# Second matmul with the weights stationary, evacuated by a transposing copy

## The chip, the cores and the metric

The kernel runs on one core of a Trainium2 chip. The metric is the device time of one execution in microseconds (us). Before the change three executions took 692.01, 692.06 and 692.52 us; the median is 692.06. TensorE (PE in the profile) multiplies, VectorE (DVE) and ScalarE (ACT) work elementwise, GpSimd (POOL) and SyncE (SP) mostly issue DMAs here. TensorE accumulates into PSUM[...]; the other tiles lie in SBUF.

## The reference

A causal convolution of 7 taps over the sequence, with weights shared within each of 8 heads, and then two matmuls with a leaky ReLU between them:

```python
# attention: x (8, 4096, 192), weight (8 heads, 7 taps)
w = softmax(weight, axis=-1)
out[b, s, h*24 + g] = sum_k w[h, k] * x_pad[b, s + k, h*24 + g]   # 6 zeros in front
# moe: tokens = out.reshape(32768, 192), w_in (192, 2048), w_out (2048, 192)
h = tokens @ w_in
g = np.maximum(0.01 * h, h)
return (g @ w_out).astype(np.float32)
```

## The kernel before

**Layout.** Two sequences are handled together: partitions 0 to 63 hold 64 channels of sequence `2*rp`, partitions 64 to 127 the same channels of `2*rp + 1`, and the 192 channels are three chunks c of 64. A block `blk` is 512 positions (`ST`) of such a pair, 1024 tokens; there are 32. The first four blocks (`NHALF`) are worked as two *half groups* of T = 256 positions each, the other 28 as one *full group* of T = 512: 36 groups, counted from 0. `xt` holds x with channels on partitions, `yt` the convolved x in the same layout, `g` the activated hidden layer with the 2048 hidden units on partitions in 16 pieces `fc` (`NFC`).

**Convolution.** `conv_jobs` gives 21 VectorE instructions per group, for each tap k and within it each chunk c: tap 0 a multiply (L187), taps 1 to 6 a multiply-add onto `yt` (L193). The last three jobs are thus tap 6 of chunks 0, 1 and 2, and a chunk of `yt` is ready when its tap 6 is done.

**First matmul.** `mm1(grp, u)` does one of 16 (full: one piece f) or 8 (half: two pieces) units of a group: for each chunk c and each sequence e a matmul with 64 rows and 128 columns of `w_in` stationary and T columns of `yt` moving (L403). The two e lie on different row halves of the array, so the pair runs side by side; I call it a round. The result `ph` (two buffers of two banks) is activated into `g` by ScalarE (L410).

**Second matmul.** It lags the first by a group. `mm2_slot(q)` issues one slot: two matmuls of 64 hidden units each (row tile `rt`), with `g` stationary and 192 columns of `w_out` moving (L429). A pair of 128-token outputs `po` takes 32 slots in two passes of 16, `rnd`; between the passes the two row tiles change banks, and `seal` is an instruction that waits for the last matmul of the first pass and for which the first of the second pass waits. `evac_o` copies a finished `po` to SBUF, on ScalarE for half groups and on VectorE for full ones (L476), and SyncE writes it to the output (L479, L484) in rows of 768 bytes. `psum_o` has four buffers, `po` among them. The last block's eight outputs are done at the end with 128 matmuls of the whole array.

**Order.** Every engine runs its instructions in the order in which the Python code issues them (`tc.manual_schedule()`). A group has T/64 steps: two units of `mm1`, then `quota[j]` slots; the convolution of the *next* group is dealt out over the steps, before a step's slots in full groups and after them in half groups:

```python
jobs = ahead[per * j : per * (j + 1)]
if T == ST:
    ...
    for job in jobs:
        job()
    jobs = []
for _ in range(quota[j]):
    mm2_slot(slot)
...
for job in jobs:
    job()
```

A half group has 4 steps of 6, 6, 6 and 3 jobs, a full one 8 steps of 2 or 3. `load_x` (L78, on GpSimd's queue) and `transpose_x` (L93, on SyncE's queue, which also carries the outputs) bring x into `xt` about two blocks ahead. The first two groups' x comes over a special path of TensorE transposes (L149, L156), and a few taps of the first groups are convolved on TensorE (L212).

## Time and profile before

| | |
|---|---|
| median of three executions | 692.06 us |
| the profiled execution | 692.51 us, of which 690.8 us are its span |
| TensorE busy / VectorE / ScalarE | 685.2 / 501.6 / 514.4 us |
| second matmul, L429 | 8064 matmuls, 387.9 us busy |
| first matmul, L403 | 3456 matmuls, 384.1 us busy |
| convolution, L193 and L187 | 735 instructions, 436.3 us busy |
| copies of the outputs, L476 | 224 on VectorE (80.1 us), 32 on ScalarE (10.2 us) |
| DMA | 53.79 MB, 78 GB/s |

Times in the profile are those of one execution. Busy time counts overlapping matmuls once per engine and the ends of matmuls are modelled, so the rows' mean durations are longer than the distance from one matmul to the next; the pace is read from starts in the timeline. Line numbers in what follows are those of the kernel before unless said otherwise.

### The profile page before, as it was taken

To read this page: it belongs to the slowest core of one execution; us is meant where nothing else is said; L and a number is where in the kernel's file an instruction comes from. 1 tells how busy PE (TensorE), PEld (TensorE's weight loads), DVE (VectorE), ACT (ScalarE), POOL (GpSimd) and SP (SyncE) were. 2 spreads that over 40 slices of the span, in tenths; PEclk is the share of its full clock that TensorE was granted. 3 is DMA by queue.
4 is the path that set the end of the run, shared out by engine and by line. 5 is a ranking of instruction groups with operands and counts; after the bars stand their busy time and mean duration, and the time that the engine had idled before them with its cause. 6 is when DMAs were issued, how large, how long until landed. Compare 5 with 4: busy or idle time off the path is not lost.

```text
span 690.8 us, 25914 instructions
## 1 busy us (share of the span) xinstructions
PE 685.2 (99%) x11708; PEld 584.0 (85%) x11708; DVE 501.6 (73%) x986; ACT 514.4 (74%) x569; POOL 148.0 (21%) x206
## 2 busy tenths in 40 slices
PE   9999999999999999999999999999999999999998
PEld 6999988888888888888888888888888888888887
DVE  5899666777777787777787777777777877777712
ACT  6888898777777777777777777777777777777771
POOL 6822222211222201222202222112222112000000
PEclk9999999999999999999999999999999999999999
DMA  9976656455565545565455566355565455322112
GB/s 151 117 93 94 82 69 84 80 78 70 75 85 82 76 77 75 66 94 82 71 78 71 74 84 88 67 78 75 77 82 80 77 75 66 67 60 59 48 42 64
DMA packets 184159, 53.79 MB, mean 78 GB/s; under 512 B 149104, under 2 KB 183664, under 8 KB 184048
## 3 DMA queue, kind: packets, MB, share of 16 engines
q0 software_dynamic: 99536, 14.76, 30.2%
q1 hardware_dynamic: 84512, 37.38, 22.8%
q8 instruction: 91, 1.49, 0.9%
q14 instruction: 20, 0.16, 0.1%
HBM read 29.88 MB, written 25.17 MB: 80 GB/s over the span
## 4 chain that ended last, share of the span: by engine, by line
PE 98%; ACT 2%; issue 0%; DVE 0%
PE po L429 49%; PE ph L403 47%; ACT g L410 2%; PE acc L212 1%; PE warm L284 1%; PE ptr L149 0%; ACT yt L371 0%; DVE o_sb L476 0%; PE ptr L156 0%; PE wps L320 0%; PE wps_l L320 0%; DVE zero L227 0%; DVE junk L229 0%
## 5 line engine op out<-in xcount | busy, mean ns | idle before, releaser
L410 ACT ACTIVATE g<-ph 128x1024 bf16<-128x1024 f32 x512 | 496.3, 1021 | 155.9 <-PE ph L403 155.4
L193 DVE SCALAR_TENSOR_TENSOR yt<-xt,wk,yt 128x512 bf16<-128x512 bf16 (+1 forms) x630 | 399.5, 691 | 0.2
L429 PEld LDWEIGHTS <-g 64*128 64x128 bf16 (+1 forms) x8064 | 361.9, 94 | 34.4 <-issue 0.2
L429 PE MATMUL po<-w_out,g 64*128 64x192 bf16 (+1 forms) x8064 | 387.9, 243 | 0.0
L403 PE MATMUL ph<-yt,w_in 64*128 64x512 bf16 (+1 forms) x3456 | 384.1, 352 | 1.5 <-ACT g L410 0.7
L403 PEld LDWEIGHTS <-w_in 64*128 64x128 bf16 x3456 | 226.0, 111 | 64.7 <-issue 3.7
L78 POOL DMA_DIRECT2D x_bf<-in_x_dram x180 | 134.6, 772 | 422.6 <-DMA xt<-x_bf 420.1
L476 DVE COPY o_sb<-po 128x192 f32<-128x192 f32 x224 | 80.1, 358 | 163.9 <-PE po L429 156.3
L187 DVE TENSOR_SCALAR yt<-xt,wk 128x512 bf16<-128x512 bf16 (+1 forms) x105 | 36.8, 381 | 12.8 <-DMA xt<-x_bf 12.6
L476 ACT COPY o_sb<-po 128x192 f32<-128x192 f32 x32 | 10.2, 320 | 1.5 <-PE po L429 0.2
L168 DVE COPY xt<-ptr 128x384 bf16<-128x384 bf16 x7 | 2.2, 354 | 6.9 <-PE ptr L156 4.5
L212 PE MATMUL acc<-xt,diag 64*64 64x256 bf16 x84 | 6.7, 327 | 0.0
L212 PEld LDWEIGHTS <-diag 64*64 64x64 bf16 x84 | 5.5, 133 | 1.3 <-DVE wk L366 0.4
L284 PE MATMUL warm<-zero 128*128 128x256 bf16 (+1 forms) x20 | 4.8, 405 | 1.1 <-DVE junk L229 1.1
L127 POOL DMA_DIRECT2D x_half<-in_x_dram x6 | 4.3, 714 | 3.2 <-DMA w_in<-in_moe_w_in_dram 3.2
L284 PEld LDWEIGHTS <-zero 128*128 128x128 bf16 x20 | 2.5, 136 | 2.1 <-DVE junk L229 1.1
L249 POOL DMA_DIRECT2D w_in<-in_moe_w_in_dram x6 | 3.9, 654 | 0.0
L371 ACT ACTIVATE yt<-acc,rsum 128x256 bf16<-128x256 f32 x3 | 1.4, 474 | 2.9 <-PE acc L212 2.9
L345 ACT ACTIVATE diag<-ident,whm 128x64 bf16<-128x64 bf16 x14 | 3.5, 335 | 0.0
L123 POOL DMA_DIRECT2D x_rows<-in_x_dram x4 | 2.9, 733 | 0.2 <-issue 0.2
L133 ACT CAST x_half<-x_nat 128x384 bf16<-128x384 f32 x2 | 1.0, 512 | 1.2 <-DMA x_nat<-in_x_dram 1.1
L290 ACT ACT_TABLE_LOAD x1 | 1.3, 1283 | 0.8 <-PEq L575 0.8
(37 smaller groups left out, 11.9 us busy)
## 6 DMA issues: line engine op xcount, KB each, us to landing
out_dram<-o_sb SPq DMA_DIRECT2D x117, 192.0 KB, 2.1
x_bf<-in_x_dram POOLq DMA_DIRECT2D x180, 64.0 KB, 3.2
out_dram<-o_sb SPq DMA_DIRECT2D x22, 96.0 KB, 1.6
xt<-x_bf SPq DMA_TRANSPOSE x90, 2.5
w_in<-in_moe_w_in_dram POOLq DMA_DIRECT2D x4, 192.0 KB, 5.8
w_in<-in_moe_w_in_dram POOLq DMA_DIRECT2D x2, 384.0 KB, 9.4
w_out<-in_moe_w_out_dram POOLq DMA_DIRECT2D x1, 768.0 KB, 11.2
x_nat<-in_x_dram SPq DMA_DIRECT2D x2, 192.0 KB, 2.6
```

What stands on the lines that cost most here:

```text
L78: nc.gpsimd.dma_start(out=t[:, c, :, e, :], in_=src[2 * rp + e, :, :, c * CH : (c + 1) * CH],)
L127: nc.gpsimd.dma_start(out=x_half[q][:, c, :, e, :], in_=rows[:, e, :, c * CH : (c + 1) * CH],)
L187: lambda s=src, d=dst, c=c: nc.vector.tensor_scalar_mul(d, s, wk[:, c, 0:1])
L193: lambda s=src, d=dst, c=c, k=k: nc.vector.scalar_tensor_tensor(out=d, in0=s, scalar=wk[:, c, k : k + 1], in1=d, op0=mybir.AluOpType.mult, ...
L212: lambda k=k, p=p, a=a, e=e, ps=ps: nc.tensor.matmul(out=acc[ps, :T], lhsT=diag[c][ps, p, k, :], rhs=xt[0][ps, c, a : a + T], start=(k == ...
L249: nc.gpsimd.dma_start(out=w_in[n][e * CH : (e + 1) * CH], in_=moe_w_in[:, fs].rearrange("(c p) f -> p c f", p=CH),)
L284: nc.tensor.matmul(out=wa[:, 0, 0:cols], lhsT=zero[:, 0:128], rhs=zero[:, 0:cols], start=True, stop=True,)
L345: nc.scalar.activation(out=diag[c][:, p, k, :], in_=ident2, func=mybir.ActivationFunctionType.Copy, scale=whm[:, c, p, k : k + 1],)
L403: nc.tensor.matmul(out=ph[:, e, i * T : (i + 1) * T], lhsT=w_in_of(f, ps, c), rhs=y[ps, c, t0 : t0 + T], start=(c == 0), stop=(c == NCH - 1),)
L410: act = nc.scalar.activation(out=g[blk][:, nf * u : nf * (u + 1), :, t0 : t0 + T], in_=ph.rearrange("p e (i t) -> p i e t", i=nf), func=my ...
L429: return nc.tensor.matmul(out=po[m], lhsT=g[b][ps, fc, e, s * 128 : (s + 1) * 128], rhs=w_out[ps, fc, :], start=start, stop=stop,)
L476: ins = copy(out=o_sb[:, n % 2, :], in_=po.pop(n))
```

## The change

The second matmul now keeps 64x64 pieces of `w_out` stationary and moves T columns of `g`. A slot issues four matmuls, for the two halves of the hidden piece (`rt`) and the two sequences (`e`), each on its own 64x64 quarter of the array. The output is transposed: `acc2[gi, r]` has on partition `64*e + m` the output channel `3*m + r` (`NR` = 3) of sequence e and T positions in a row. A group takes three passes of 16 slots, 48 in all; the two row tiles are always on different r, r = 1 is finished after the second pass, r = 0 and r = 2 after the third. After passes one and two `seal`, now always a ScalarE copy of one element, lies between.

`evac_t` takes an `acc2` to SBUF with VectorE's transposing copy of 32x32 blocks, into a tile `o_t` that has positions on partitions; with the third, four DMAs write the group's output in runs of 96 channels (384 bytes). The first matmul's matmuls are split in two of 64 columns each (`h`), so that both matmuls use the same 64x64 tiles. `g_pool` goes from three buffers to two. The quotas are written out: half groups 16, 16, 8, 8; full groups 5, 5, 6, 5, 5, 6, 8, 8; groups 6 to 8 have their own. The last block keeps its matmuls.

```diff
-    g_pool = ctx.enter_context(tc.tile_pool(name="g", bufs=3))
+    g_pool = ctx.enter_context(tc.tile_pool(name="g", bufs=2))
...
-                    nc.tensor.matmul(
-                        out=ph[:, e, i * T : (i + 1) * T],
-                        lhsT=w_in_of(f, ps, c),
...
+                    for h in range(2):
+                        nc.tensor.matmul(
+                            out=ph[h * CH : (h + 1) * CH, e, i * T : (i + 1) * T],
+                            lhsT=w_in_of(f, ps, c, h),
...
+    def w_out_of(ps, fc, r):
+        return w_out[ps, fc, r::NR]
 
     def mm2_slot(q):
...
-        p, fc = divmod(q, 2 * NFC)
+        gi, fc = divmod(q, NR * NFC)
         rnd, fc = divmod(fc, NFC)
...
+        if first:
+            for r in ((1, 0), (2,), ())[rnd]:
+                acc2[gi, r] = psum_o.tile([128, ST], FP32, name="acc2", tag="po")
         for rt in range(2):
+            r = (rnd + rt) % NR
+            fresh = (rnd, rt) in ((0, 0), (0, 1), (1, 1))
+            done = (rnd, rt) in ((1, 0), (2, 0), (2, 1))
+            b, t0, T = groups[gi]
+            ps = slice(rt * CH, (rt + 1) * CH)
+            for e in range(2):
+                ins = nc.tensor.matmul(
+                    out=acc2[gi, r][e * CH : (e + 1) * CH, 0:T],
+                    lhsT=w_out_of(ps, fc, r),
+                    rhs=g[b][ps, fc, e, t0 : t0 + T],
+                    start=first and fresh,
+                    stop=last and done,
+                )
+                if first and not fresh:
+                    sync(ins, seal, "the other row tile has left this bank")
+        if last and rnd < 2:
+            seal = nc.scalar.copy(out=junk, in_=junk)
+            sync(seal, ins, "between the rounds")
+        if last and rnd > 0:
+            for r in ((), (1,), (0, 2))[rnd]:
+                evac_t(gi, r)
+
+    def evac_t(gi, r):
+        b, t0, T = groups[gi]
+        if gi not in osb:
+            osb[gi] = o_pool.tile([128, ST // GB, GB, NR], FP32, name="o_t")
+        nc.vector.transpose(
+            out=osb[gi][:, 0 : T // GB, :, r],
+            in_=acc2.pop((gi, r))[:, 0:T].rearrange("p (j k) -> p j k", k=GB),
+        )
+        if r != 2:
+            return
...
+        for e in range(2):
...
+            for h in range(2):
+                p = (2 * e + h) * GB
+                nc.sync.dma_start(
+                    out=rows[:, :, h * NR * GB : (h + 1) * NR * GB],
+                    in_=t[p : p + GB, 0 : T // GB].rearrange("p j k r -> p j (k r)"),
+                )
...
+    half = [16, 16, 8, 8]
+    full = [5, 5, 6, 5, 5, 6, 8, 8]
     plan = {
-        2 * NHALF - 2: [16, 8, 8, 16],
-        2 * NHALF - 1: [8, 8, 16, 16],
-        2 * NHALF: [16, 8, 8, 16, 8, 8, 16, 16],
+        0: [0] * 4,
+        2 * NHALF - 2: [16, 8, 8, 8],
+        2 * NHALF - 1: [8, 8, 8, 16],
+        2 * NHALF: [8] * 8,
     }
```

## The prediction

> **What bounds the kernel now.** I read the page from the chain downwards, then the rows of the two matmul lines, then the timeline for the pace of each engine. First the chain of work that ended last, by engine and by line:

> ```profile
> PE 98%; ACT 2%; issue 0%; DVE 0%
> PE po L429 49%; PE ph L403 47%; ACT g L410 2%; PE acc L212 1%; PE warm L284 1%; PE ptr L149 0%; ACT yt L371 0%; DVE o_sb L476 0%; PE ptr L156 0%; PE wps L320 0%; PE wps_l L320 0%; DVE zero L227 0%; DVE junk L229 0%
> ```

> TensorE is the bound, half of it in the second matmul (L429), half in the first (L403). Whatever makes TensorE wait is paid in full. The rows (busy, mean ns | idle before, releaser):

> ```profile
> L410 ACT ACTIVATE g<-ph 128x1024 bf16<-128x1024 f32 x512 | 496.3, 1021 | 155.9 <-PE ph L403 155.4
> L193 DVE SCALAR_TENSOR_TENSOR yt<-xt,wk,yt 128x512 bf16<-128x512 bf16 (+1 forms) x630 | 399.5, 691 | 0.2
> L429 PE MATMUL po<-w_out,g 64*128 64x192 bf16 (+1 forms) x8064 | 387.9, 243 | 0.0
> L403 PE MATMUL ph<-yt,w_in 64*128 64x512 bf16 (+1 forms) x3456 | 384.1, 352 | 1.5 <-ACT g L410 0.7
> L476 DVE COPY o_sb<-po 128x192 f32<-128x192 f32 x224 | 80.1, 358 | 163.9 <-PE po L429 156.3
> L476 ACT COPY o_sb<-po 128x192 f32<-128x192 f32 x32 | 10.2, 320 | 1.5 <-PE po L429 0.2
> ```

> See that L403 waited only 1.5 us in the whole run, and that the 32 evacuations of the eight half groups were on ScalarE, so VectorE had nothing of TensorE's to wait for there. Durations overlap, so the pace comes from the timeline (start, us, engine, line, count), here half groups, then full groups:

> ```profile
> 69.16 1.51 PE L403 MATMUL ph<-yt,w_in 64*128 64x256 bf16 x24
> 70.47 1.52 PE L429 MATMUL po<-w_out,g 64*128 64x192 bf16 x32
> 71.79 1.51 PE L403 MATMUL ph<-yt,w_in 64*128 64x256 bf16 x24
> ...
> 237.66 1.49 PE L403 MATMUL ph<-yt,w_in 64*128 64x512 bf16 x12
> 238.96 1.52 PE L429 MATMUL po<-w_out,g 64*128 64x192 bf16 x32
> 240.28 1.49 PE L403 MATMUL ph<-yt,w_in 64*128 64x512 bf16 x12
> ```

> Start to start: 24 first matmuls of 256 columns in 1.31 us are 12 rounds of two row tiles, 109 ns each; 12 of 512 columns in 1.295 us are 6 rounds of 216 ns; 16 slots of the second matmul take 1.32 us, 82.5 ns each. A step is 2.63 us (half) or 2.615 us (full), a half group 10.5 us, a full one 20.9 us.

> Last, VectorE's convolution for the group ahead:

> ```profile
> 65.73 7.21 DVE L193 SCALAR_TENSOR_TENSOR yt<-xt,wk,yt 128x256 bf16<-128x256 bf16 x18
> ...
> 79.32 12.01 DVE L193 SCALAR_TENSOR_TENSOR yt<-xt,wk,yt 128x512 bf16<-128x512 bf16 x18
> 97.62 12.01 DVE L193 SCALAR_TENSOR_TENSOR yt<-xt,wk,yt 128x512 bf16<-128x512 bf16 x18
> ```

> 18 in a row go at 0.396 us (256 columns; the last needs its 0.478) and 0.662 us (512; 0.745). The chain at 79.32 is that of group 8, whose first matmul starts at 93.33: VectorE runs most of a group ahead.

> [...]the 64*64 transposes of L156, four tiles of 64 columns each, start their rounds 32 ns apart, while one matmul's row says 193 ns. So two column tiles read one row half side by side, and four 64-column weight loads fit in 32 ns. [...]VectorE's queue is strictly first in, first out; L476 agrees, 156 us of waiting with the conv queued behind. [...]

> **The change, part by part.**

> *Second matmul.* Removed: 3968 slots x 82.5 ns = 327.4 us. Added: 35 groups x 48 slots of four 64x64 tiles. At the round times above, 8 half groups x 48 x 109 ns = 41.9 and 27 full ones x 48 x 215.8 ns = 279.6, 321.5 us. **Minus 5.8 us**, all on the bounding engine. The last block keeps its 128 matmuls. Unknown: whether a round of four costs as much as one of two. The L156 round is 2.5 ns above two rows' overhead; over 1680 rounds here and 1728 of the first matmul that would be 8 us. [...]nothing shows that, so I take 0.

> *First matmul.* Each L403 matmul becomes two (6912), in the same 1728 rounds: 0. It brings both matmuls into one tiling mode[...].

> *Evacuation.* Away: 216 VectorE and 32 ScalarE copies. New: three VectorE transposing copies per group, no row shows one. [...]I estimate 0.42 us (256) and 0.69 us (512); in a row 0.08 less, as the copies of L476 overlap. [...] VectorE's sum falls in full groups (2.1 us for 2.9), but *order* matters. A transposing copy waits for TensorE, and the conv of the next group is queued behind it.

> *Full groups.* Conv jobs of a step precede its slots. The r=1 copy waits for step 5's end; behind it are 6 conv jobs: 0.4 signal + 0.6 + 6 x 0.662 + 0.1 = 5.1 us, against two steps of 1.295 + 8 x 0.216 = 6.05 us. It fits by 1 us (0.4 with the slow copy): 0.

> *Half groups 1 to 5.* Here the jobs follow the slots, six per step. From the end E of round 1 (step 1) VectorE's queue is: copy r=1, 12 jobs, copies r=0 and 2, and three last jobs, which are the last tap of the *next* group's three chunks. The first is done at 0.30 (the 269 ns of a 256-column matmul and 0.03 of signal) + 0.34 + 12 x 0.396 + 0.68 + 0.51 (0.478 and 0.03) = 6.58 us; the others 0.4 apart. TensorE wants it after one round and steps 2 and 3: 0.11 + 2 x (1.31 + 8 x 0.109) = 4.48 us. It waits 2.10, then 0.29 twice: 2.68 x 5 = **13.4 us**. That the two copies also want slot 47 hides nothing: TensorE is done before.

> *Group 6.* r=1 falls at the end of step 2, with 6 jobs in front of the three: 0.30 + 0.34 + 2.38 + 0.51 = 3.53 against 2.29: 1.24 + 0.58 = **1.8 us**.

> *Group 7.* Step 0 ends group 5's last round, so both its copies stand ahead of group 8's full-size conv: 0.30 + 0.68 + 3 x 0.27 + 15 x 0.662 + copy 0.34 + 0.78 = 12.84, against 0.11 + 2 x 2.18 + 3.06 = 7.53 us of TensorE. It waits 5.3, then 0.45 twice: **6.2 us**. Before, VectorE was a group ahead here. The gap may halve the clock for a time; 0 to 4 us, I add none.

> *The rest.* The two seals become ScalarE copies of one element, placed at step ends; 1.3 us of first matmul stands between them and the round that needs them, and ScalarE has 16 x 0.92 us of work in 20.7: 0. If that cover went, each would cost some 0.3 us. g from three buffers to two: the slots of a group are done before the group after next writes: 0. SyncE issues four output DMAs per group in pieces of 384 B for 768 B; a 768 B packet takes 39 ns of one engine, and 63,488 packets even at 39 ns are 2.5 ms of 16 x 690 us, 22%, where DMA stands at 54% with half of that: no bound. The x transposes on SyncE's queue now stand behind outputs that wait for VectorE; block 5's follow within 3 us of group 7's first step, 7 us to landing, and VectorE needs them 10 us later: hidden.

> Sum: 692.5 (span 690.8 and 1.7 around it) - 5.8 + 13.4 + 1.8 + 6.2 = 708.1. The profiled execution lies 0.4 above the median of 692.06; I say **708.0**.

> **Rivals.** *Rounds of four cost more* (chance 0.18): 2.5 ns per round, 716; what speaks for it is the 32 ns round, against it that weight load and switch lie under 109 or 216 ns of columns, and that L212's 64*64 rounds take 109 ns too. *The transposing copy runs at half rate* (0.12): three copies x 0.27 us in seven boundaries, about 5 us: 713. *VectorE's chain fits*, the case on the other side (0.06): if the wait at the half-group boundary is nil only the 5.8 us remain, 687. It decides where the chain of 6.6 us drops under 4.5, and for a net gain the boundaries would have to cost under 5.8 together instead of 21; the job pace of 0.396 us is measured, so only another order of the queue could do it. *Tiles that don't run together* (0.02): two column tiles taking turns would double 3408 rounds, above 1200; L156 excludes it at 64 columns. The case above: 0.62.

> **The numbers.** A measurement of this kernel can tell about 0.2%, 1.4 us. Faster 0.06 is the case on the other side; 0.02 for the same is what lies between it and the rest; slower 0.92. The range of 702 to 721 takes in [...]slow copies, the clock or most of the round's extra above.

> **What would show it.** The steps: L403 idle for "DVE yt" of about 21 us, with five pieces of 2 us and one of 5 us between 30 and 120 us; from then on no waits, full groups at 20.7 us; conv rows broken by the transposing copy. I am wrong if the half groups show no such idle time, if a full group takes over 20.9 us, or if the transposing copy of 512 columns is far from 0.7 us.

## The result, and the profile after

The changed kernel takes **713.13 us** (four executions, 711.49 to 715.13) against 692.29 for the kernel before beside it: 1.030 times as long, 95% interval 1.026 to 1.033. The prediction was 708.0 in a range of 702 to 721. The profiled execution took 711.49 us with a span of 709.8, 19.0 more than before. The executions differ in the mean clock that TensorE was granted: 711.49 us at 0.998, 712.03 at 0.995, 714.23 at 0.992, 715.13 at 0.990.

First the page, by the same parts as before; the lines are numbered by the changed kernel (L400 first matmul, L446 second, L195 convolution, L468 transposing copy):

```profile
PE 91%; DVE 6%; DMA 1%; POOL 1%; issue 0%; ACT 0%; POOLq 0%
...
L400 PE MATMUL ph<-yt,w_in 64*64 64x512 bf16 (+1 forms) x6912 | 397.2, 354 | 18.8 <-DVE yt L195 14.5
...
L446 PE MATMUL acc<-g,w_out 64*64 64x512 bf16 (+1 forms) x6720 | 379.1, 352 | 0.4 <-issue 0.4
```

VectorE has entered the chain with 6%, and L400, which had waited 1.5 us, waits 18.8, most of it for the convolution. The waits of the changed kernel (engine, line, waited for: us, times, longest) say the same:

```profile
DVE o_t L468 <- PE acc L446: 200.1, 65, 13.1
...
PE ph L400 <- DVE yt L195: 14.5, 7, 5.1
PEld L400 <- issue: 8.5, 24, 1.6
...
PE ph L400 <- issue: 1.4, 1, 1.4
```

PEld is TensorE's loading of weights. "Issue" is time in which an engine waited for nothing that the profile shows. PE waits seven times for the convolution, as many times as there are boundaries from group 1 to group 8. The timeline shows one of them, before group 5, on TensorE and on VectorE:

```profile
72.92 1.10 PE L446 MATMUL acc<-g,w_out 64*64 64x256 bf16 x32
75.95 2.10 PE L400 MATMUL ph<-yt,w_in 64*64 64x256 bf16 x48 [1.93 <-DVE yt L195]
```

```profile
69.61 0.54 DVE L468 STREAM_TRANSPOSE o_t<-acc 128x256 f32<-128x256 f32 x1 [4.43 <-PE acc L446]
70.03 4.78 DVE L195 SCALAR_TENSOR_TENSOR yt<-xt,wk,yt 128x256 bf16<-128x256 bf16 x12
74.72 0.87 DVE L468 STREAM_TRANSPOSE o_t<-acc 128x256 f32<-128x256 f32 x2
75.46 1.23 DVE L195 SCALAR_TENSOR_TENSOR yt<-xt,wk,yt 128x256 bf16<-128x256 bf16 x3
```

This is the queue of the prediction, instruction by instruction. VectorE idles 4.43 us for r = 1, then has 12 jobs, two copies and the three jobs that group 5 needs; the first is done at 75.9 and TensorE goes on at 75.95. VectorE had the time: it spent it waiting. From the last round of group 4, at 73.75 in the trace, to the first of group 5 are 2.20 us, so 2.09 are lost beyond the 0.11 of a round; the idle time in the list is less because it counts from a matmul's modelled end.

Where the time went, from the first matmul of one group to that of the next (us):

| group | before | after | difference |
|---|---|---|---|
| 1, 2, 4, 5 | 11.13, 10.52, 10.52, 10.52 | 13.82, 13.29, 13.28, 13.28 | +2.69, +2.77, +2.76, +2.76 |
| 3 | 10.52 | 14.32 | +3.80 |
| 6, 7 | 9.45, 9.45 | 11.60, 15.62 | +2.15, +6.17 |
| 8 | 18.82 | 19.53 | +0.71 |
| 9 | 20.92 | 20.81 | -0.11 |
| 10 to 34, each | 20.92 | 20.72 | -0.20 |

Groups 1 to 7 lose 23.1 us and group 8 another 0.7, groups 9 to 34 win back 5.1. In a full group the pace of TensorE is this:

```profile
350.61 1.52 PE L400 MATMUL ph<-yt,w_in 64*64 64x512 bf16 x24
351.91 1.30 PE L446 MATMUL acc<-g,w_out 64*64 64x512 bf16 x20
352.99 1.52 PE L400 MATMUL ph<-yt,w_in 64*64 64x512 bf16 x24
```

The 24 first matmuls, six rounds of four, take 1.30 us from start to start and the 20 second ones, five rounds, 1.08: 216 ns a round in both.

### The profile page after: what moved, and what is told of

The parts are those of the page before. It is cut to its first block, busy times and chain, and to the rows that moved or that the text cites. A ratio compares the mean times of both kernels' runs of the same rounds, so it can differ in the third digit from the quotient of the medians.

```text
span 709.8 us, 30177 instructions
## 1 busy us (share of the span) xinstructions
PE 685.3 (97%) x13948; PEld 610.5 (86%) x13948; DVE 492.4 (69%) x875; ACT 517.5 (73%) x606; POOL 147.0 (21%) x206
## 3 DMA queue, kind: packets, MB, share of 16 engines
q8 instruction: 109, 1.79, 1.1%
## 4 chain that ended last, share of the span: by engine, by line
PE 91%; DVE 6%; DMA 1%; POOL 1%; issue 0%; ACT 0%; POOLq 0%
PE ph L400 45%; PE acc L446 44%; DVE yt L195 5%; PE po L489 2%; DMA w_in<-in_moe_w_in_dram 1%; DVE o_t L468 1%; POOL w_in L251 0%; ACT g L407 0%; POOL x_rows L125 0%; POOL sel L236 0%; DVE yt L189 0%; DVE o_sb L501 0%; POOL ident masks.py:199 0%; PE ptr L151 0%; POOL sel L234 0%
## 5 line engine op out<-in xcount | busy, mean ns | idle before, releaser
L407 ACT ACTIVATE g<-ph 128x1024 bf16<-128x1024 f32 x512 | 496.5, 1021 | 163.0 <-PE ph L400 162.6
L400 PE MATMUL ph<-yt,w_in 64*64 64x512 bf16 (+1 forms) x6912 | 397.2, 354 | 18.8 <-DVE yt L195 14.5
L195 DVE SCALAR_TENSOR_TENSOR yt<-xt,wk,yt 128x512 bf16<-128x512 bf16 (+1 forms) x630 | 388.4, 690 | 0.2
L446 PE MATMUL acc<-g,w_out 64*64 64x512 bf16 (+1 forms) x6720 | 379.1, 352 | 0.4 <-issue 0.4
L400 PEld LDWEIGHTS <-w_in 64*64 64x64 bf16 x6912 | 311.8, 133 | 51.2 <-DVE yt L195 16.3
L446 PEld LDWEIGHTS <-w_out 64*64 64x64 bf16 x6720 | 284.5, 118 | 39.2 <-issue 1.0
L468 DVE STREAM_TRANSPOSE o_t<-acc 128x512 f32<-128x512 f32 (+1 forms) x105 | 79.0, 792 | 200.1 <-PE acc L446 200.1
L456 ACT COPY junk<-junk 128x1 f32<-128x1 f32 x70 | 13.5, 192 | 11.4 <-PE acc L446 7.0
L489 PEld LDWEIGHTS <-g 128*128 128x128 bf16 x128 | 10.5, 98 | 0.4 <-issue 0.4
L489 PE MATMUL po<-w_out,g 128*128 128x192 bf16 x128 | 10.7, 246 | 0.0
L501 DVE COPY o_sb<-po 128x192 f32<-128x192 f32 x8 | 2.7, 352 | 6.8 <-PE po L489 6.1
```

Of the source, the lines that this page charges most:

```text
L195: lambda s=src, d=dst, c=c, k=k: nc.vector.scalar_tensor_tensor(out=d, in0=s, scalar=wk[:, c, k : k + 1], in1=d, op0=mybir.AluOpType.mult, ...
L400: nc.tensor.matmul(out=ph[h * CH : (h + 1) * CH, e, i * T : (i + 1) * T], lhsT=w_in_of(f, ps, c, h), rhs=y[ps, c, t0 : t0 + T], start=(c = ...
L407: act = nc.scalar.activation(out=g[blk][:, nf * u : nf * (u + 1), :, t0 : t0 + T], in_=ph.rearrange("p e (i t) -> p i e t", i=nf), func=my ...
L446: ins = nc.tensor.matmul(out=acc2[gi, r][e * CH : (e + 1) * CH, 0:T], lhsT=w_out_of(ps, fc, r), rhs=g[b][ps, fc, e, t0 : t0 + T], start=fi ...
L456: seal = nc.scalar.copy(out=junk, in_=junk)
L468: nc.vector.transpose(out=osb[gi][:, 0 : T // GB, :, r], in_=acc2.pop((gi, r))[:, 0:T].rearrange("p (j k) -> p j k", k=GB),)
```

## The experiments

The theory to be tested (A): the loss is the order of VectorE's queue at the half-group boundaries, and the four-tile form itself is a small gain. The rivals: the four-tile rounds or the transposing copy are slow by themselves; the split of the first matmul costs something.

### The jobs before the slots

```diff
             if T == ST:
                 jobs = ahead[len(ahead) * j // steps : len(ahead) * (j + 1) // steps]
+            if i > 0:
                 for job in jobs:
                     job()
                 jobs = []
```

> The changed kernel with one thing undone of its order: in half groups the convolution jobs of a step are issued before its slots, as in full groups. Theory A (the loss is VectorE's queue: the last conv jobs stand behind transposing copies that wait for TensorE): the six half-group boundaries lose their 2 us waits, the gap before group 8 shrinks from 5.1 to about 2.5 us, and the time falls by some 20 us to 686 to 690, below the kernel before, since the full groups keep 20.72 us. Rival B (the four-tile rounds or the transposing copy themselves cost the time): stays within 3 us of 712.

Measured: 700.36 us, 1.012 times the kernel before (1.010 to 1.014). That is 12.8 us less than the changed kernel, so the order of the queue is the larger part; the waits for the convolution before groups 2 to 7 are gone, and that before group 8 is 2.0 us. The full groups keep 20.72 us. But A had asked for some 20 us less, a time of 686 to 690, and groups 2 to 7 still take 71.2 us together where the kernel before takes 61.0. Of these 10.2 us, 2.0 are the wait before group 8. Most of the rest has another name, here in the waits of this kernel:

```profile
PEld L400 <- issue: 8.8, 16, 2.1
...
PE ph L400 <- issue: 3.7, 4, 1.9
```

In groups 2 to 7 the weight loads pause nine times, for 0.3 to 1.2 us and once for 2.1, some 7 us in all, at distances of about 4, 8 or 12 us. The page's DMA table has a queue of kind "instruction", q8, with 91 packets of 16 KB before and 109 after, 1.49 and 1.79 MB. TensorE's 11708 and 13948 pairs of weight load and matmul make 64 bytes an instruction in both, so q8 fits TensorE's program, 256 instructions to a packet. A round of four tiles is eight instructions. In 109 ns that is 73 per us, and a packet of 256 lasts 3.5 us; in the half groups of the kernel before it was four in 109 or in 82.5 ns, 37 or 48 per us by turns. That TensorE has to wait for its instructions is theory I, tested below.

### The kernel before, with its half-group copies on VectorE

```diff
-        copy = nc.scalar.copy if b < NHALF else nc.vector.tensor_copy
+        copy = nc.vector.tensor_copy
```

> The kernel before with one line changed: the output copies of the half groups go to VectorE, as in full groups; no four-tile matmul and no transposing copy. Theory A: the same fault appears without the change, waits of 1.3 to 1.6 us at each half-group boundary and about 4 us before group 8, together 15 us more: about 707. Rival B: within 2 us of 692, for 32 copies of 0.36 us are hidden.

Measured: 709.49 us, 1.025 times the kernel before (1.023 to 1.026). One line, no four-tile matmul and no transposition, and most of the loss is there. Its timeline has the boundary, on TensorE:

```profile
66.85 1.52 PE L429 MATMUL po<-w_out,g 64*128 64x192 bf16 x32
69.23 2.07 PE L403 MATMUL ph<-yt,w_in 64*128 64x256 bf16 x24 [0.87 <-DVE yt L193]
```

A half group goes from 10.52 to 12.15 us, 1.63 more, and the gap before group 8 is 3.4 us. After that gap TensorE's granted clock is 0.50 in the first 5.7 us of group 8, which takes 3.0 us more than before. So such a loss needs neither four-tile rounds nor a transposition: a queue in order and a copy that waits for TensorE suffice. That the four-tile rounds are free in the half groups is not shown by this; what the jobs-first kernel has left over speaks against it.

### The first matmul left whole

```diff
-                    for h in range(2):
-                        nc.tensor.matmul(
-                            out=ph[h * CH : (h + 1) * CH, e, i * T : (i + 1) * T],
-                            lhsT=w_in_of(f, ps, c, h),
+                    nc.tensor.matmul(
+                        out=ph[:, e, i * T : (i + 1) * T],
+                        lhsT=w_in_of(f, ps, c),
...
```

> The changed kernel with the first matmul left at 128 columns, so that TensorE goes from 64x128 tiles to 64x64 tiles and back in every step. Prediction's reading: the split of the first matmul is free[...]; where the kernel before changes between such tiles (at L156) about 0.09 us go, so some 500 changes cost about 45 us: 750 to 760. Rival C: [...]the split was not needed: 710 to 715. Rival D: the split costs something itself, 6912 matmuls for 3456: below 710.

Measured: 772.43 us, 1.116 times the kernel before (1.114 to 1.118). The timeline of the weight loads shows why: each change between the two tile shapes leaves the loads idle, here for 0.40 to 0.41 us.

```profile
301.46 1.01 PEld L399 LDWEIGHTS <-w_in 64*128 64x128 bf16 x12 [0.40 <-issue]
302.88 0.82 PEld L445 LDWEIGHTS <-w_out 64*64 64x64 bf16 x20 [0.41 <-issue]
304.10 1.01 PEld L399 LDWEIGHTS <-w_in 64*128 64x128 bf16 x12 [0.40 <-issue]
```

A full group takes 22.83 us for 20.72: 2.11 us for 16 changes, 0.13 each. Splitting the first matmul is thus a necessary part of the change, and in the full groups it is free. What holds the loads back at a change is not shown.

### The transposing copy without its step

```diff
-            out=osb[gi][:, 0 : T // GB, :, r],
+            out=osb[gi][:, r * T : (r + 1) * T].rearrange("p (j k) -> p j k", k=GB),
...
```

> The changed kernel with the transposing copy writing its 256 or 512 values side by side instead of 12 bytes apart; the output is then out of order in the rows. If the step of 12 bytes is what makes the copy 0.87 us instead of the estimated 0.69, the rows fall to 0.69 and 0.42 us and the time by 1 to 3 us; if the transposition itself is slower[...], they stay at 0.87 and 0.52 us.

The copies by shape, in the changed kernel and then in this one:

```profile
L468 DVE STREAM_TRANSPOSE o_t<-acc 128x512 f32<-128x512 f32 x81 | 67.6, 873 | 166.5 <-PE acc L446 166.5
L468 DVE STREAM_TRANSPOSE o_t<-acc 128x256 f32<-128x256 f32 x24 | 11.4, 518 | 33.6 <-PE acc L446 33.6
```

```profile
L468 DVE STREAM_TRANSPOSE o_t<-acc 128x512 f32<-128x512 f32 x81 | 54.8, 703 | 175.8 <-PE acc L446 175.8
L468 DVE STREAM_TRANSPOSE o_t<-acc 128x256 f32<-128x256 f32 x24 | 9.8, 434 | 36.3 <-PE acc L446 36.3
```

Side by side the copy takes what was estimated, 0.70 and 0.43 us; the 12-byte step adds 0.17 and 0.08. The shorter copies are worth little: before groups 3, 5 and 6 TensorE idles 1.87 us for 1.93, 0.06 less, and VectorE waits longer for TensorE instead. The single time, 712.72 us, lies within the spread of the changed kernel and can't show so small a gain, for the mean granted clock was 0.993. The trace of this execution shows what lies behind such a mean, here on TensorE at the start of group 4 (a row of the windows ends with the granted clock, the DMA share and GB/s):

```profile
62.36 3.15 PE L400 MATMUL ph<-yt,w_in 64*64 64x256 bf16 x48 [1.87 <-DVE yt L195]
```

```profile
62.63:66.04 3.41, 3.35 (x64) 3.03 (x63) 2.24 (x8) 1.51 (x2) 0.62 (x1) 0.50 1.35 156
```

After a wait of 1.87 us the clock is halved for 3.4 us, and group 4 takes 14.59 us, 1.31 more than in the changed kernel's trace. The same happens after the wait of 1.45 us before group 2, which takes 1.60 more, and after the gap before group 8. The waits before groups 3, 5 and 6, as long as that before group 4, are not followed by it.

### Full groups at the half groups' instruction rate

```diff
+                for z in range(0, T, HT):
...
-                            out=ph[h * CH : (h + 1) * CH, e, i * T : (i + 1) * T],
+                                out=ph[h * CH : (h + 1) * CH, e, i * T + z : i * T + z + HT],
...
+        for z in range(0, T, HT):
...
-                    out=acc2[gi, r][e * CH : (e + 1) * CH, 0:T],
+                        out=acc2[gi, r][e * CH : (e + 1) * CH, z : z + HT],
```

> The changed kernel with every 512-column matmul of the two lines made of two of 256 columns: TensorE takes twice the instructions per column in the full groups, the rate that the half groups have. Theory I (instruction supply: 16 KB pieces of TensorE's program, 256 instructions, last 3.5 us at this rate and come every 3.7 to 4.2 us in the half groups of the run with the jobs first): pauses of 0.3 to 1 us now appear in the full groups too, a full group takes 22.5 to 25 us, and the time is above 750. Rival (the pauses in the half groups come from something else there, the DMA load of the start or the waits around): a full group takes 20.97 us, for 2.5 ns more per 512 columns, and the time is about 719.

One execution: 797.33 us. Its program's queue and its chain:

```profile
q8 instruction: 191, 3.13, 1.7%
...
PE 86%; issue 7%; DVE 5%; DMA 1%; POOL 1%; ACT 0%; POOLq 0%
```

"Issue" takes 7% of the chain, having been 0%. The timeline of TensorE in a full group:

```profile
354.63 0.93 PE L448 MATMUL acc<-g,w_out 64*64 64x256 bf16 x26
355.86 0.64 PE L448 MATMUL acc<-g,w_out 64*64 64x256 bf16 x14 [0.30 <-issue]
356.24 1.58 PE L401 MATMUL ph<-yt,w_in 64*64 64x256 bf16 x48
357.55 1.58 PE L448 MATMUL acc<-g,w_out 64*64 64x256 bf16 x48
358.86 0.71 PE L401 MATMUL ph<-yt,w_in 64*64 64x256 bf16 x18
360.98 1.09 PE L401 MATMUL ph<-yt,w_in 64*64 64x256 bf16 x30 [1.41 <-issue]
```

Between pauses the rounds keep 109 ns (48 matmuls in 1.31 us). The pauses break off a matmul line in its middle, where no other engine is waited for. Between the two shown lie 14 + 48 + 48 + 18 = 128 matmuls, with their loads 256 instructions: one packet. That holds throughout. The trace has 87 pauses of TensorE of over 0.15 us that are put down to issue, and the number of matmuls from any of them to any other is a multiple of 128, which a pause for another cause would have no reason to keep; in the jobs-first kernel the same is true of its six, and in the changed kernel of its two. Each of the 87 ends 2.2 to 3.2 us after a 16 KB packet of q8 has started and 1.2 to 1.6 us after it has ended. A full group takes 23.9 us in the mean, 4.0 for each of its six packets, where columns alone would give an estimated 20.96 (the 20.72 of the changed kernel, and 2.5 ns for each of 96 rounds: in the kernel before 12 rounds of 256 columns take 1.31 us, 6 of 512 take 1.295). So TensorE runs out of instructions at 73 per us. It does not pause at 37 per us, in the full groups of the changed kernel, nor in the kernel before, where 37 and 48 take turns and the mean is 43. Why the packets don't come sooner was not tried.

### Half groups as before, full groups as changed

The second matmul, the copies and the quotas of the half groups are those of the kernel before, up to the end of group 8; the first matmul is split from group 9 on.

```diff
-                mm1(grp, u)
+                mm1(grp, u, 1 if i <= 2 * NHALF else 2)
...
-                mm2_slot(slot)
+                if slot < NOLD:
+                    old_slot(slot)
+                else:
+                    mm2_slot(slot - NOLD + 2 * NHALF * NR * NFC)
```

`old_slot` is the slot of the kernel before with its copies on ScalarE, `NOLD` the number of its slots, 512.

> Half groups exactly as in the kernel before (first matmul at 128 columns, second with g stationary, copies on ScalarE), the changed form only for the second matmul of the full groups, whose first matmul is split from group 9 on. Theory A with its two parts (VectorE's queue, and since the run with the jobs first a second one: TensorE waits for its instructions in the half groups): nothing is lost up to group 9, which starts at 112 us as before, and 27 full groups at 20.72 for 20.92 us save 5.4: 687 to 688. Rival: the four-tile form costs something by itself that the half groups did not show alone: above 690.

Measured: **687.65 us**, 0.9925 times the kernel before (0.991 to 0.994), the fastest kernel of this study. Two stretches of the windows, a full group and a half group (length; busy and count of TensorE, its weight loads, VectorE, ScalarE, GpSimd; clock, DMA share, GB/s):

```profile
350.00:370.70 20.70, 20.70 (x392) 13.18 (x384) 15.03 (x25) 15.87 (x19) 4.46 (x6) 1.00 0.59 78
44.00:54.50 10.50, 10.50 (x228) 10.50 (x225) 10.50 (x29) 9.03 (x12) 3.04 (x5) 1.00 0.78 89
```

TensorE is busy throughout in both. Group 9 starts at 112.6 us, and before at 112.1; the gain comes from the full groups alone.

## Why the prediction was right, step by step

*Minus 5.8 us in the second matmul*: right in the full groups. One went from 20.92 to 20.72 us, the 0.20 of the working, so a round of four tiles costs what one of two did. The rival of dearer rounds is out, and with it tiles that don't run together.

*The split is free and brings both matmuls to one tile shape*: right in the full groups, which take 20.72 us with it; the changes of shape that it avoids are worth 59 us, 772.43 for 713.13.

*The half-group boundaries*: right, in cause and size. For the first chunk 2.10 us were forecast: TensorE loses 2.09 to 2.10 before groups 3, 5 and 6, counted between the starts of rounds, and for the other two chunks 0.29 each, as forecast. Before groups 2 and 4 it loses 1.4, because it comes to the boundary late itself: in group 3 it pauses, for a reason given below; in group 1, which also has transposes of x to do, the reason was not looked for. The waits at the ends of *groups 6 and 7* were forecast at 1.24 and 5.3 us and are 1.28 and 5.22. Counted in this way, with the later chunks, all seven boundaries cost 20.0 of the 21.4 us forecast; the 14.5 us in the list of waits are less because the list leaves out the later chunks and counts from modelled ends.

*The transposing copy at 0.42 and 0.69 us*: mis-sized, 0.52 and 0.87. The two figures were the author's estimate. The rows and the timeline of the kernel before give the same: 358 ns for a copy of 192 values, and 1.04 ns for each value more if a copy goes as the convolution does, 0.396 us for 256 and 0.662 for 512. The estimate left out the 12-byte step of the output. It falls on the boundaries as 0.06 us each, as the side-by-side copy shows, and is hidden in the full groups, as the working had it for a slow copy. By the prediction's own signs, a copy far from 0.7 us would have spoken against it; 0.87 is off by a quarter, and did not matter.

*Nothing for the rest*: here the sum fell short, 15.6 us for 19.0 in the profiled execution. Two things were missing in it. One is the supply of instructions, which the prediction did not consider: it took a round of four to cost what one of two costs and asked only about columns and weight loads, not about instructions per us. In the changed kernel a half group needs 768 instructions for its matmuls and loads, three packets, and takes 13.3 us with its wait for VectorE; at some 4 us a packet that is nearly always time enough, and the supply shows in only two pauses of over 0.15 us, 0.38 us in group 1 and 1.38 in group 3. The latter makes the wait at the next boundary shorter, so that group 3 is 1.0 us longer than its neighbours. The two causes thus hide behind each other. The run with the jobs first takes one away and uncovers the other, and that is why it gave 12.8 us and not 20. The other thing is the clock, which the prediction named, at 0 to 4 us, and added as none; this too was the author's estimate, and no wait in the profile before shows it. The gap before group 8 is followed by this stretch of the windows:

```profile
112.00:116.00 4.00, 0.00 (x0) 0.00 (x0) 4.00 (x8) 0.00 (x0) 2.01 (x3) 1.00 0.37 45
116.00:120.00 4.00, 3.52 (x36) 1.81 (x40) 4.00 (x8) 1.28 (x2) 2.44 (x4) 0.57 1.32 87
```

After 5.1 us without a matmul the granted clock is 0.50 for 3.4 us, from 116.5 to 119.9 in the trace (0.57 in the mean of the second row), and rounds of 512 columns take 0.43 us. Shorter waits were followed by the same: one of 2.0 us before group 8 in the jobs-first kernel, and two of 1.45 and 1.87 us with the side-by-side copy. Other waits of 1.9 us were not, so the length of the wait alone does not decide it. Group 8 takes 19.53 us for the 18.2 of the working (eight times 1.295, 64 rounds of 0.109 and twice 0.45), and 1.0 of the difference lies in its first step, 4.1 us for 3.1.

The other executions of the changed kernel have no trace. A stretch of 3.4 us at half clock takes 0.0024 off the mean of 710 us, so their clocks of 0.995, 0.992 and 0.990 would be some two, three and four such stretches where the profiled one has one; this is an estimate. At the 1.3 to 1.6 us that each cost in the trace of the side-by-side copy, three more would make 3.9 to 4.8 us; the executions differ by 3.6. In the jobs-first kernel the clock is 0.997 to 1.000, in the last one 0.999 to 1.000.

The range held, and the direction and the mechanism were the ones named. In the profiled execution the pause in group 3 and the clock in group 8 make 2.0 of the 3.4 us that the sum fell short; the rest is spread over several groups and the end and was not taken apart. The median lies another 1.6 us higher. The clock is the likely reason, but without a trace of those executions that is not shown.

## What to carry to other kernels

When an evacuation moves to another engine or becomes an instruction that waits for TensorE, look at what stands behind it in that engine's queue and who needs that next; the sum of the busy times says nothing of it (VectorE's fell here). When a matmul is cut into more tiles, count TensorE's instructions per microsecond besides its columns: 43 per us in the mean ran without a pause here, 73 did not. When one cause of a loss is removed, look for a second that it covered. A form that gains in one stage can be kept to that stage: here it lost in the half groups, and gave 0.75% when used in the full groups alone.
